# In an attention step, ScalarE copies the turned exponentials of two steps ago before it takes the last step's exponentials

## The chip, the cores and the metric

The kernel runs on one core of a Trainium2 chip. The metric is the device time of one execution in microseconds (us). A core has five engines that each work through a queue of their own in order: TensorE (PE, with its weight loads shown apart as PEld), VectorE (DVE), ScalarE (ACT), GpSimd (POOL) and SyncE (SP), which here only issues DMAs. Results of TensorE go to PSUM banks; everything else lies in SBUF.

## The reference: window attention, then a top-1 mixture of experts

Attention: 8 batches of 8 heads, 576 positions, head size 64. A query sees itself and the 63 positions before it:

```
scores = q @ k.T / 8, masked to 0 <= i - j < 64
attn   = exp(scores - max) / (sum + 1e-9)
x      = attn @ v            # 4608 rows of 512 after heads are joined
```

Mixture of experts: `logits = x @ w_gate` (8 experts), each row goes to its best expert, and gets `gate * relu(x @ w1[e]) @ w2[e]` with 1024 hidden columns.

## The kernel before

**Attention** comes first (about the first 160 us). It is cut into 36 steps of 128 rows, two chunks of 64 positions with all eight heads; q, k and v of a chunk are loaded into a ring of 18 slots by SP. The program is written out by hand as one loop over a step number i (lines 831 to 903), and in each turn of it the parts of several steps stand side by side:

- `scores(i)` (L401, L404): PE writes the scores of step i into one of two double banks `s_b`.
- `folded(i)`, `largest(i)` (L411 to L420): DVE folds the two halves of the window into one block, and takes the negated row maxima `mxs`.
- `exps(i - 1)` (L428): ACT takes the exponentials of the step before, eight activations of 128x64, one a head, from `s_b` into the tile `pf`.
- `transp(i - 1)` (L433): PE turns them, four transposes into the one bank `t_b`.
- `evac(i - 2)` (L437): ACT copies `t_b`, with the turned exponentials of two steps ago, into the tile `tsb`.
- `apart(i - 2)` (L444): POOL multiplies `tsb` by two masks and so writes the two tiles `pm`, two instructions.
- `values(i - 3)` (L458): PE multiplies `pm` with v into the bank pair `x_b`; the first product of a head needs the first `pm`, the next one the second.
- `shares(i - 3)` (L464 to L468): DVE divides by the row sums into `xrow`, and SP writes that out.
- `rows_t(i - 4)`, `cols_t(i - 4)` (L475, L482): PE turns `xrow` of the step before that, and ACT copies it to `xT`, for the gate's logits, which follow every fourth step (L519).

On PE the order within a turn is scores, values, `rows_t`, `transp`, and every fourth time the logits. On DVE it is folding, maxima, shares, and after them pieces of the routing (L534 to L603) and, late in the phase, the low parts of the first experts' weights (`wlo`, L237). On ACT it is the exponentials, the copy of `t_b`, the copy of `xT`, and small pieces behind it (`whi`, L240). `t_b` is one bank: the transposes of a turn wait until the copy of the step before has been taken out of it. `s_b`, `pf`, `tsb` and `pm` each have two buffers.

**The experts** follow (160 us to the end): passes of 256 or 384 gathered rows through an expert's two matrices, on PE without a break, each product made of three with the values split into a high and a low part. From turn 36 on the first of these passes are interleaved with what is left of the attention.

The change touches only the order of three calls in the loop.

Of the kernel before, what the change touches and what calls it, by code (L numbers as in the profile page):

```python
# [118 lines left out]
def window_attention_then_top1_moe(ctx: ExitStack, tc: tile.TileContext, qkv, wall, wg, cst, out):  # L119
# [66 lines left out]
    def turn(t, u, xt, b=None):  # L186
        xh, xl = xt
        xp = (bank("xp") if b is None else b).rearrange("p (k t) -> p k t", k=4)
        for kk in range(4):
            nc.tensor.transpose(xp[:, kk], t[:, u, kk * P:(kk + 1) * P], ident)  # L190
        us = slice(u * P, (u + 1) * P)
        nc.scalar.copy(out=xh[:, :, us], in_=xp)
        nc.vector.tensor_tensor(out=xl[:, :, us], in0=xp, in1=xh[:, :, us], op=ALU.subtract)  # L193
# [3 lines left out]
    class Weights:  # L197
# [11 lines left out]
        def load(self):  # L209
            jj = self.loaded  # L210
            if jj == NJ // 2:
                return
            self.loaded += 1
            raw = self.raws[jj] = wr.tile([P, 2, 2 * C], F32, name="raw")
            ev = self.ev
            src = wall[ev, jj] if isinstance(ev, int) else wall[bass.ds(ev, 1), jj].rearrange("o p j f -> p (o j) f")
            if jj < self.spread:
                at, gap = QUARTERS[jj]
                quarters.extend((at + gap * k, raw[:, k // 2, k % 2 * C:(k % 2 + 1) * C],
                                 src[:, k // 2, k % 2 * C:(k % 2 + 1) * C]) for k in range(4))  # L220
            else:
                nc.sync.dma_start(out=raw, in_=src)
# [157 lines left out]
    def keep_busy(k):  # L380

        for _ in range(k):
            nc.tensor.matmul(x_b[:, 1].rearrange("p (k t) -> p k t", k=4), lhsT=ones, start=True, stop=True,
                             rhs=ones.unsqueeze(1).to_broadcast([P, 4, P]))
# [375 lines left out]
    def table(lo, hi):  # L760
        read(gathered(keep["said"], NT, hi - lo, t_b), hi - lo, idx_sb[:, lo:hi], gate_sb[:, lo:hi])
# [8 lines left out]
    def get(i):  # L770
        fetch(xg[i % 3], cols(idx_sb, passes[i]))

    def flip(i, blocks=None):
        for u in range(len(passes[i])) if blocks is None else blocks:
            if u == 0:
                xt[i] = columns(xw)
            if u < len(passes[i]):
                turn(xg[i % 3], u, xt[i])

    def open_weights(i):  # L780
        wts[i] = Weights(expert_of(passes[i][0]))

    def each(f, n):
        if 0 <= n < NS:
            f(n)
# [17 lines left out]
    def do(what):  # L803
        if rs_[what]:
            rs_[what], f = None, rs_[what]
            f()
# [3 lines left out]
    def forward(i, place):  # L810
        if i >= TURN:
            for _ in range(FORWARD[i > TURN][place]):
                next(early)

    def split_ahead():

        w = next((ew[e] for e in range(EARLY) if e in ew and ew[e].given < NJ), None)
        if w and not w.ready:
            w.ready.append(w.split_(lows=lows))

    def single(k):
        sp = ctx.enter_context(tc.tile_pool(name=f"sp{k}", bufs=1, space=PSUM, side=side[k]))
        return [sp.tile([P, C], F32, name=f"e_b{2 * k + h}") for h in range(2)]

    def due(i):
        while begin and begin[0][0] <= i:
            begin.popleft()[1]()

    with tc.manual_schedule():
        keep_busy(BUSY[0])  # L830
        for i in range(NS + LAST):
            for c in range(FIRST, 2 * NS):

                if c % 2 and i == (c - RING + 1) // 2 + 4:
                    load(c)
            if i == LOADW:
                ew[0] = Weights(0, len(QUARTERS))
            if i == SPLIT:
                ew[0].prepare(AHEAD, pieces)
            if i == TURN:  # L840
                ew[0].first = ew[0].split()

            rs_["step"] = i
            if slow and slow[0][0]:
                f = slow.popleft()[1]
                if f:
                    f()
            if i <= TURN:
                due(i)
            each(exps, i - 1)  # L850
            each(evac, i - 2)
            each(apart, i - 2)
            if i == TURN:
                scored[1].close()
                turns["hp"] = single(1)
            while exs:
                exs.popleft()()
            if i > 5 and settled:
                settled.popleft()()
            if i > TURN:  # L860
                split_ahead()
            forward(i, 0)
            do("first")
            each(scores, i)
            each(folded, i)
            each(largest, i)
            if i < len(BUSY) - 1:
                keep_busy(BUSY[i + 1])
            forward(i, 1)
            each(values, i - 3)  # L870
            if i > TURN:
                due(i)
            for c in range(FIRST, 2 * NS):
                if c % 2 == 0 and i == (c - RING) // 2 + 3:
                    load(c)
            if quarters and quarters[0][0] <= i:
                _, o, w = quarters.popleft()
                nc.sync.dma_start(out=o, in_=w)
            if rs_["fast"] and (rs_["fast"][0][0] < i):
                rs_["fast"].popleft()[1]()  # L880
            forward(i, 2)
            each(rows_t, i - 4)
            each(cols_t, i - 4)
            forward(i, 3)
            each(transp, i - 1)
            do("last")
            each(shares, i - 3)
            do("read")
            if i == TURN - 1:
                scored[0].close()  # L890
                turns.update(xp=[t_b], yp=single(0))
                for u in range(2):
                    turn(xg[0], u, xe[0], turns["yp"][u])
            for k in range(RATE[0] if i < NS else 4):
                if slow and not slow[0][0]:
                    slow.popleft()[1]()
            for k in range(RATE[1] if i < NS else 4):
                if puts and not slow:
                    puts.popleft()()
            while lows:  # L900
                lows.popleft()()
            if pieces:
                pieces.popleft()()
        assert not (rs_["fast"] or slow or begin), (len(rs_["fast"]), len(slow), len(begin))
        while puts:
            puts.popleft()()
        st.close()
        xw = ctx.enter_context(tc.tile_pool(name="xw", bufs=2))
        xn = ctx.enter_context(tc.tile_pool(name="xn", bufs=1))
        turns["xp"].append(m_b)  # L910
        turns["yp"] = [x_b[:, 0], x_b[:, 1], *turns["yp"]]


        def steps():
            for _ in plan():
                for _ in range(WAIT[0]):
                    yield
            for _ in range(WAIT[1]):
                yield
            table(0, NMA)  # L920
            while "turned" not in keep:
                yield
            get(0)
            yield
            open_weights(0)
            get(1)

        rest = steps()
        for e, j in early:
            next(rest, None)  # L930
            if e == EARLY - 1 and j == NJ - 3:
                for _ in rest:
                    pass
            if e == EARLY - 1 and j is not None and j >= NJ - 3:
                flip(0, [j - NJ + 3])
# [62 lines left out]
```

## Time and profile before

| | |
|---|---|
| median of 3 runs | 649.79 us (648.19 to 986.33) |
| the profiled execution | 648.77 us, of which the span from first to last instruction is 647.0 us |
| PE busy, span | 612.2 us, 95% |
| ACT, DVE, POOL busy | 361.8, 397.5, 196.9 us |
| mean granted TensorE clock | 0.995 |

A row of a timeline gives the start, the duration, the engine, the line of the kernel and the operation with its output and input; several instructions of a kind that follow each other are one row (x64). In brackets stands how long the engine was idle before, and what ended that. Where it says "issue", the profile shows nothing that the engine waited for.

### The profile page before, as it was taken

Reading aid. Unit: us, or ns where it says so; the run is one execution under the profiler, and the core shown is the slowest. Engines: PE = TensorE matmul, PEld = TensorE weight load, DVE = VectorE, ACT = ScalarE, POOL = GpSimd, SP = SyncE. Lnnn points to the kernel's source line nnn. Section 1 sums busy time; section 2 is a strip of 40 time slices with the busy share of each in tenths; the row PEclk is TensorE's granted clock in tenths of the full one; section 3 lists DMA queues with packets and bytes.
Section 4 is the critical chain, followed back from the end, with each engine's and each line's share of the span. In section 5 each row is a group of like instructions: output and inputs, shape, how many; then the busy total and the mean of one; then the engine's idle time right before and its main releaser. Section 6 shows DMA issues by size and latency. Waiting matters only on the chain.

```text
span 647.0 us, 16938 instructions
## 1 busy us (share of the span) xinstructions
PE 612.2 (95%) x6995; PEld 542.6 (84%) x6995; DVE 397.5 (61%) x707; ACT 361.8 (56%) x763; POOL 196.9 (30%) x180
## 2 busy tenths in 40 slices
PE   8799988888989999999999999999999999999995
PEld 4688877777877899899899999999999999999994
DVE  4566769976789665744455556556556565655651
ACT  4576767675444455635345565565655655566551
POOL 4666657675521331401113122121211211111011
PEclk9999999999999999999999999999999999999999
DMA  9988888952645668634546666665666666555521
GB/s 304 345 274 263 295 262 264 314 172 100 247 146 194 212 206 296 221 137 140 180 162 224 218 224 235 204 223 208 226 226 210 223 236 225 210 182 187 212 98 34
DMA packets 35110, 138.13 MB, mean 213 GB/s; under 512 B 4940, under 2 KB 6092, under 8 KB 25552
## 3 DMA queue, kind: packets, MB, share of 16 engines
q1 hardware_dynamic: 28624, 118.08, 53.6%
q0 software_dynamic: 6400, 18.88, 8.4%
q8 instruction: 57, 0.93, 0.6%
q14 instruction: 29, 0.24, 0.1%
HBM read 119.11 MB, written 19.92 MB: 215 GB/s over the span
## 4 chain that ended last, share of the span: by engine, by line
PE 74%; DVE 12%; issue 9%; ACT 2%; POOL 2%; another core or an unknown queue 0%; POOLq 0%; DVEq 0%; ACTq 0%
PE e_b L307 20%; PE e_b L278 14%; PE x_b L278 14%; PE e_b L311 10%; PE x_b L458 4%; PE s_b L401 4%; DVE wlo L237 2%; PE m_b L475 2%; DVE s_b L418 1%; DVE s_b L412 1%; DVE xrow L468 1%; PE m_b L519 1%; PE t_b L190 1%; PE t_b L433 1%; PE m_b L190 1%
## 5 line engine op out<-in xcount | busy, mean ns | idle before, releaser
L237 DVE TENSOR_TENSOR wlo<-raw,whi 128x1024 fp32r<-128x1024 f32 (+1 forms) x158 | 188.6, 1194 | 165.7 <-ACT whi L240 153.1
L240 ACT CAST whi<-raw 128x1024 fp32r<-128x1024 f32 (+1 forms) x153 | 155.1, 1015 | 106.6 <-PE x_b L278 54.8
L307 PE MATMUL e_b<-xh,whi 128*128 128x256 f32 (+1 forms) x480 | 127.2, 294 | 0.0
L307 PE MATMUL e_b<-xl,whi 128*128 128x256 f32 (+1 forms) x480 | 125.0, 289 | 0.2 <-DVE xl L193 0.2
L444 POOL TENSOR_TENSOR pm<-tsb,cs 128x512 f32<-128x512 f32 x72 | 90.4, 1278 | 55.3 <-ACT tsb L437 48.5
L317 ACT ACTIVATE hh<-e_b 128x256 fp32r<-128x256 f32 (+1 forms) x152 | 60.4, 397 | 82.2 <-PE e_b L311 79.1
L307 PEld LDWEIGHTS e_b<-xl,whi 128*128 128x128 f32 x480 | 90.8, 189 | 4.1 <-DVE xl L193 0.6
L307 PEld LDWEIGHTS e_b<-xh,whi 128*128 128x128 f32 x480 | 90.8, 189 | 3.6
L267 POOL DMA_INDIRECT out<-ys,idx_sb x32 | 38.4, 1201 | 177.5 <-ACT ys L266 173.0
L179 POOL DMA_INDIRECT xg<-xs,idx_sb x32 | 35.2, 1099 | 180.9 <-PE m_b L190 127.9
L311 PE MATMUL e_b<-xh,wlo 128*128 128x256 f32 (+1 forms) x480 | 79.7, 288 | 0.0
L318 DVE SCALAR_TENSOR_TENSOR hl<-e_b,hh 128x256 fp32r<-128x256 f32 (+1 forms) x152 | 65.6, 432 | 15.3 <-ACT hh L317 14.7
L428 ACT ACTIVATE pf<-s_b,mxs 128x64 f32<-128x64 f32 x288 | 63.1, 339 | 9.7 <-DVE mxs L420 7.9
L311 PEld LDWEIGHTS e_b<-xh,wlo 128*128 128x128 f32 x480 | 67.7, 188 | 0.0
L278 PE MATMUL x_b<-whi,hh 128*128 128x512 f32 x160 | 62.9, 393 | 0.8 <-ACT ys L266 0.8
L278 PE MATMUL e_b<-whi,hl 128*128 128x512 f32 x160 | 62.8, 393 | 0.6 <-DVE hl L318 0.6
L278 PE MATMUL x_b<-whi,hl 128*128 128x512 f32 x160 | 62.8, 392 | 0.3 <-DVE hl L318 0.2
L278 PE MATMUL x_b<-wlo,hh 128*128 128x512 f32 x160 | 62.8, 393 | 0.0
L278 PE MATMUL e_b<-wlo,hh 128*128 128x512 f32 x160 | 62.8, 393 | 0.0
L278 PE MATMUL e_b<-whi,hh 128*128 128x512 f32 x160 | 62.7, 392 | 0.0
L458 PE MATMUL x_b<-ring,pm 64*64 64x65 f32 x2176 | 48.2, 224 | 14.1 <-issue 8.5
L458 PEld LDWEIGHTS x_b<-ring,pm 64*64 64x64 f32 x2176 | 42.5, 135 | 20.0 <-issue 13.9
(160 smaller groups left out, 886.6 us busy)
## 6 DMA issues: line engine op xcount, KB each, us to landing
raw<-wall SPq DMA_DIRECT2D x74, 1024.0 KB, 5.4
ring<-qkv SPq DMA_DIRECT2D x66, 386.0 KB, 4.4
xs<-xrow SPq DMA_DIRECT2D x36, 256.0 KB, 3.8
raw<-wall SPq DMA_DIRECT2D x8, 256.0 KB, 5.9
ring<-qkv SPq DMA_DIRECT2D x4, 256.0 KB, 4.8
ring<-qkv SPq DMA_DIRECT2D x4, 130.0 KB, 5.1
ring<-qkv SPq DMA_DIRECT2D x1, 512.0 KB
xg<-xs,idx_sb POOLq DMA_INDIRECT x32
```

The costliest lines, as they stand in the source:

```text
L179: nc.gpsimd.indirect_dma_start(out=t[:, u], out_offset=None, in_=xs[0:rows], in_offset=bass.IndirectOffsetOnAxis(ap=ix, axis=0), bounds_ch ...
L237: nc.vector.tensor_tensor(out=lo[:, s], in0=raw[:, s], in1=hi[:, s], op=ALU.subtract)
L240: nc.scalar.copy(out=hi[:, s], in_=raw[:, s])
L267: ins = nc.gpsimd.indirect_dma_start(out=out, out_offset=bass.IndirectOffsetOnAxis(ap=ix, axis=0), in_=ys, in_offset=None, bounds_check=N ...
L278: nc.tensor.matmul(y, lhsT=x[:, us], rhs=w[:, C:], start=(j == 0 and m == 0), stop=(j == NJ - 1 and m == 2))
L307: nc.tensor.matmul(hp[:, 0:w], lhsT=hi[:, ks], rhs=x[:, kk, 0:w], start=(kk == 0 and x is xh), stop=False)
L311: nc.tensor.matmul(hp[:, 0:w], lhsT=lo[:, kk * P:(kk + 1) * P], rhs=xh[:, kk, 0:w], start=False, stop=(kk == 3))
L317: nc.scalar.activation(out=hh[:, 0:w], in_=hp[:, 0:w], func=AF.Relu)
L318: nc.vector.scalar_tensor_tensor(out=hl[:, 0:w], in0=hp[:, 0:w], scalar=0.0, in1=hh[:, 0:w], op0=ALU.max, op1=ALU.subtract)
L428: nc.scalar.activation(out=pf[:, g, a], in_=sp[:, a, g, 0], func=AF.Exp, bias=mx[:, h:h + 1], scale=SCALE)
L444: nc.gpsimd.tensor_tensor(out=pm[i], in0=t.rearrange("p (g q) -> p g q", g=NG), op=ALU.mult, in1=cc("mask")[:, i * P:(i + 1) * P].unsqueez ...
L458: nc.tensor.matmul(x_b[cols, a, g * V1:(g + 1) * V1], lhsT=pm[i][rows, g, cols], rhs=v_r[rows, c % RING - i, g], start=(i == 0), stop=(i = ...
```

## The change

The copy of `t_b` and the two multiplications behind it are called ahead of the exponentials.

```diff
             if i <= TURN:
                 due(i)
-            each(exps, i - 1)
             each(evac, i - 2)
             each(apart, i - 2)
+            each(exps, i - 1)
             if i == TURN:
                 scored[1].close()
```

ACT's queue in a turn is then: the copy of `t_b`, the eight exponentials, the copy of `xT`. No instruction is added or taken away, and no other engine's queue has another order.

## Rows read from the trace of the kernel before

**Rows 1.** The page's first part: busy us, share of the span, instructions.

```profile
PE 612.2 (95%) x6995; PEld 542.6 (84%) x6995; DVE 397.5 (61%) x707; ACT 361.8 (56%) x763; POOL 196.9 (30%) x180
```

**Rows 2.** Stretches of 10 us: busy us (instructions) by engine, clock, DMA share, GB/s.

```profile
20.00:30.00 10.00, 6.24 (x190) 5.31 (x192) 5.55 (x14) 5.63 (x21) 5.62 (x5) 0.97 1.00 383
...
70.00:80.00 10.00, 9.62 (x306) 8.21 (x308) 7.93 (x21) 8.12 (x30) 6.13 (x5) 1.00 0.87 294
...
120.00:130.00 10.00, 8.90 (x246) 7.85 (x248) 9.17 (x21) 7.65 (x29) 6.18 (x5) 1.00 0.92 310
```

**Rows 3.** Waits in the first 175 us: us in total, times, longest.

```profile
POOL pm L444 <- ACT tsb L437: 48.5, 26, 8.0
...
PE x_b L458 <- POOL pm L444: 2.8, 4, 0.9
...
ACT tsb L437 <- PE t_b L433: 0.3, 1, 0.3
```

**Rows 4.** Timeline of ACT in one attention step.

```profile
77.31 0.59 ACT L482 COPY xT<-m_b 128x512 f32<-128x512 f32 x1 [0.75 <-PE m_b L475]
77.80 1.76 ACT L428 ACTIVATE pf<-s_b,mxs 128x64 f32<-128x64 f32 x8
79.38 0.65 ACT L437 COPY tsb<-t_b 128x512 f32<-128x512 f32 x1
```

**Rows 5.** Timeline of POOL in that step, and in one at 124 us.

```profile
80.11 2.51 POOL L444 TENSOR_TENSOR pm<-tsb,cs 128x512 f32<-128x512 f32 x2 [0.96 <-ACT tsb L437]
...
123.92 2.75 POOL L444 TENSOR_TENSOR pm<-tsb,cs 128x512 f32<-128x512 f32 x2 [3.00 <-ACT tsb L437]
```

**Rows 6.** Timeline of PE: values and transposes of several steps.

```profile
15.27 1.03 PE L458 MATMUL x_b<-ring,pm 64*64 64x65 f32 x40 [0.78 <-POOL pm L444]
...
18.68 1.04 PE L458 MATMUL x_b<-ring,pm 64*64 64x65 f32 x56 [0.57 <-POOL pm L444]
...
44.75 1.42 PE L458 MATMUL x_b<-ring,pm 64*64 64x65 f32 x64 [0.49 <-DVE xrow L468]
...
48.49 1.15 PE L458 MATMUL x_b<-ring,pm 64*64 64x65 f32 x61 [0.17 <-issue]
...
64.10 1.11 PE L458 MATMUL x_b<-ring,pm 64*64 64x65 f32 x64
...
75.21 1.48 PE L458 MATMUL x_b<-ring,pm 64*64 64x65 f32 x64
...
77.11 0.60 PE L433 MATMUL t_b<-cs,pf 128*128 128x128 f32 x4
...
78.87 1.38 PE L458 MATMUL x_b<-ring,pm 64*64 64x65 f32 x64
...
80.67 0.60 PE L433 MATMUL t_b<-cs,pf 128*128 128x128 f32 x4
...
112.86 1.27 PE L458 MATMUL x_b<-ring,pm 64*64 64x65 f32 x64
...
126.73 1.03 PE L458 MATMUL x_b<-ring,pm 64*64 64x65 f32 x40 [0.91 <-POOL pm L444]
```

**Rows 7.** Stretches of 1 us around the longest stall, columns as in Rows 2.

```profile
28.00:29.00 1.00, 0.00 (x0) 0.00 (x0) 0.34 (x2) 0.09 (x1) 1.00 (x1) 1.00 1.04 324
29.00:30.00 1.00, 0.46 (x17) 0.46 (x20) 0.00 (x0) 0.00 (x0) 1.00 (x2) 0.68 0.69 273
...
32.00:33.00 1.00, 1.00 (x16) 0.67 (x18) 0.00 (x0) 1.00 (x5) 0.00 (x0) 0.61 0.73 222
```

**Rows 8.** The chain that ended last: start, us, what.

```profile
125.55 1.41 DVE wlo L237
```

**Rows 9.** DVE by shape, 85 to 165 us: count, busy us, mean ns, idle.

```profile
L603 DVE TENSOR_TENSOR hot_row<-rowb,lo 128x512 bf16<-128x512 bf16 x7 | 5.3, 777 | 0.1
L237 DVE TENSOR_TENSOR wlo<-raw,whi 128x256 fp32r<-128x256 f32 x8 | 5.1, 638 | 0.1
```

**Rows 10.** Timeline of DVE: the same instruction twice.

```profile
121.75 0.42 DVE L237 TENSOR_TENSOR wlo<-raw,whi 128x256 fp32r<-128x256 f32 x1
...
125.48 1.48 DVE L237 TENSOR_TENSOR wlo<-raw,whi 128x256 fp32r<-128x256 f32 x1
```

## The prediction, made before the changed kernel was built or run

> **What bounds the kernel now.** I read the page first. PE is busy for 95% of the span [rows 1], and the change touches only the attention steps, some 160 of 647 us, so what it can be worth is read there. The table of busy time by stretches comes next [rows 2]; three regimes are to be seen in it. From 20 to 30 us the DMA engines are full (share 1.00) and PE has work for only 6.24 of 10 us. From 70 to 80 us PE is busy for 9.62 us and nothing else is close. From 120 to 130 us DVE is at 9.17 and PE at 8.90.
>
> Then the list of waits [rows 3]. POOL waits 48.5 us for the copy of the turned exponentials, which looks like much, but POOL's idleness is no cost by itself. What PE shows as a wait for POOL's masked tiles is 2.8 us in four places; that is the number the change can work on.
>
> Last the timelines, of one step. ACT copies `xT` at 77.31, takes eight exponentials from 77.80 and copies `t_b` at 79.38 [rows 4], although the transposes that filled `t_b` ended at 77.71 (77.11 and 0.60) [rows 6]. So the copy lies ready for 1.67 us and waits its turn. POOL follows at 80.11 and is done at 82.62 [rows 5]. The values of a step take 1.11 us on PE where nothing holds them (64.10), and 1.38 and 1.48 us in the steps around 75 and 79 [rows 6]: in the middle of them PE waits for the second masked tile. Such short waits are too small for the list, and I count them below.
>
> **The change, part by part.** One ACT copy of 0.65 us moves ahead of eight activations of 1.76 us together [rows 4]. Nothing is added or removed. The two POOL instructions move in program text with it, but no other POOL instruction stands between the old and the new place, so POOL's order is the same; SP, DVE and PE are not touched either, and no DMA is issued in what is moved.
>
> *What comes earlier.* The copy starts when the transposes have ended, or the `xT` copy ahead of it: 77.80 in the step shown, not 79.38, so 1.58 us earlier. The masked tiles come earlier by as much wherever POOL waits for the copy. No wait of PE for the second tile in rows 6 that I can see in a plain step is longer than 1.58 us, so all of them go, as far as something else is not late next.
>
> *The first steps.* PE waits 0.78 us at 15.27 and 0.57 us at 18.68 [rows 6], 1.35 us together. But the next 10 us are those with full DMA engines and a PE that is idle for over a third [rows 2]. A PE that arrives earlier there waits longer for what the DMAs bring. The bounds are 0 and 1.35 us; I take 0.4, nearer to the lower end, since the share of 1.00 says that the transfers set the pace.
>
> *The stretch where PE sets the pace, 40 to 115 us.* The excess over 1.11 us is 0.31 (44.75), 0.04 and an idle 0.17 (48.49), 0.37 (75.21), 0.27 (78.87) and 0.16 (112.86) [rows 6]: 1.3 us. Other steps are within 0.1 us of the 1.11. I take 1.3, with 0.6 as the lower bound (half, if DVE's rows of the step before hold the values next, as they do for 0.49 us at 44.75).
>
> *The stretch where DVE sets the pace, 85 to 105 and 120 to 150 us.* At 126.73 PE waits 0.91 us for POOL [rows 6], but the chain of what ended last runs over DVE there (the 1.41 us at 125.55) [rows 8], so I count nothing; the cover is DVE's own work, and without it this would be 0.9 us more of gain.
>
> *What comes later.* The exponentials end later by the copy ahead of them, 0.49 us from start to start if that is spaced as 77.31 to 77.80, at most 0.65. Who waits: the transposes at the end of the same PE turn. In the step shown the exponentials end at 79.56 and would end at 80.05 to 80.21; the transposes start at 80.67 [rows 4, 6]. If the values ahead of them lose their 0.27 us of waiting, they start at 80.40, so 0.2 to 0.35 us are left. The transposes wait today for the copy and the exponentials both, whichever is last, and their sum on ACT is the same. Taken at nothing; the bounds are 0 and the whole 1.3 us (it can give the gain back, not more, because in the old order the same two pieces end at 80.03).
>
> *The new wait.* The copy now stands at the head of ACT's turn and can hold the exponentials back until PE has finished the transposes. They ended at 77.71 and ACT became free at 77.80; and where they were late before, the copy waited 0.3 us in one place of 36 [rows 3]. Behind it on ACT stand eight exponentials and the `xT` copy; with the slack above this costs nothing, at most 0.1 us a step over the 11 or so tightest ones, 1 us.
>
> *DVE and POOL side by side.* The same `wlo` instruction takes 0.42 us at 121.75 and 1.48 us at 125.48 [rows 10]; POOL's masking ran from 123.92 to 126.67 [rows 5], and the slow one ended soon after it. So one of the two holds the other up, and the change shifts POOL by 1.6 us against DVE. The Trainium skill, SBUF — State Buffer, "Who interferes with whom", says that a DVE instruction with two inputs in SBUF and a GpSimd instruction that reads SBUF exclude each other for a whole instruction; by that rule alone the sum could come out on the other side, and it is the third case below. The trace agrees: 1.06 us is near what is left of a masking instruction of about 1.26 us, half of 2.51. From the rows: 15 such instructions (8 `wlo`, 7 `hot_row`) took 10.4 us [rows 9]; at 0.42 and, for `hot_row`, my estimate of 0.69 (its mean of 0.777 less about 0.09 for the one or two that look held) they would take 8.2, so 2.2 us are paid today. Bounds: the 2.2 go, or each of 15 waits half a masking instruction, 0.63 us, 9.4 in all, 7.2 more than today. I take no change: at 121.6 the copy would start in place of the exponentials and POOL at about 122.3, when the `wlo` of 121.75 has just ended, and the one of 125.48 would find POOL done; elsewhere it can go the other way.
>
> *Sum.* 0.4 + 1.3 = 1.7 us less than the profiled execution's 648.77 (span 647.0): 647.1 us. That execution stands 1.0 us below the median shown and 0.6 above the lowest run, so I hold it for typical.
>
> **The rivals.** (1) *Nothing reaches the end.* DMA takes the front, DVE and the exponentials take the rest: 648.8 us. For it speaks that the end of the exponentials has only 0.2 to 0.35 us of slack, against it the plain excess in steps where PE has nothing else to wait for.
>
> (2) *More goes than I count.* The whole 1.35 of the front, 1.3, the 0.9 at 126.73, and the 2.2 of DVE: 5.8 us, 643.0. Also the clock: after the stall at 28 us, in which PE ran nothing, the granted clock fell to 0.68, and it was 0.61 in the fourth 1 us stretch from there [rows 7]; if the stall shrinks so that the fall does not come, the missing shares of two of these stretches alone are 0.7 us, near 1.5 for the four as an estimate. Then 641.5. A fall more costs as much: 648.6 in my forecast.
>
> (3) *POOL collides with DVE: slower.* Place: 85 to 165 us, where after the shares DVE has its two-input instructions. They come at the end of DVE's turn, and POOL's two instructions would now start about 0.75 us after the transposes, where today they start 2.4 us after them. The price is 0.63 us for each of 15, 7.2 us over today, less the 1.7: 654.3. It decides where such an instruction starts after POOL has, not before. In the step at 121.75 it is before by some 0.1 us; that is thin. For over 2% each would have to wait for a whole masking instruction: 15 x 1.26 is 18.9, less 2.2 and 1.7 gives 15 us, 663.8; little speaks for that.
>
> **How the numbers follow.** Forecast (645 to 648): 0.48. Rival 1 (648 to 650): 0.22. Rival 2 (640 to 645): 0.15. Rival 3 (650 up): 0.15. The time is the forecast's, 647.1. The range leaves out the lower part of rival 2 and the upper of rival 3, about 0.1 each, and so goes from 642.0 to 652.0. 2%, about what a measurement tells from no change, is 13 us; below it I see 0.015 (all of rival 2 twice over) and above it 0.02 (rival 3 at full price). Within: 0.965.
>
> **What would show it.** In the changed kernel's timeline the copy of `t_b` starts where the exponentials do now, POOL starts within 0.8 us of the end of the transposes, and POOL's wait for the copy shifts, not shrinks. PE's listed wait for POOL, 2.8 us, goes to under 1, and values of a plain step take 1.11 us. The plain step from transposes to transposes, 3.56 us at 77 to 81, should be near 3.3. I am wrong if PE waits for exponentials in many steps (rival 1), if the two-input instructions of DVE take clearly more than 10.4 us together (rival 3), or if the attention phase as a whole ends over 4 us earlier (rival 2).

## The result, and the profile after it

The changed kernel takes 657.39 us in the median of 4 runs (655.74 to 659.93); the kernel before, run beside it, 649.45. The ratio is 1.0148, with an interval of 1.0124 to 1.0172: 1.5% slower by this ratio, 1.2% by the two medians, where 647.1 us and a range of 642 to 652 were forecast. The ratios leave out two executions that stand far off, one of the kernel before (986.33 us) and one of an experiment (1511.14 us). A second series gave 1.0149 [1.0108, 1.0191]. The profiled execution took 658.86 us (span 657.0), 10.1 more than the profiled one before.

ACT does what was intended. Its timeline in a step of the changed kernel (columns as in [rows 4]):

```profile
46.74 0.59 ACT L482 COPY xT<-m_b 128x512 f32<-128x512 f32 x1 [0.90 <-PE m_b L475]
47.23 0.59 ACT L437 COPY tsb<-t_b 128x512 f32<-128x512 f32 x1
47.72 1.55 ACT L428 ACTIVATE pf<-s_b,mxs 128x64 f32<-128x64 f32 x7
```

The copy starts 0.09 us after the transposes (46.54 + 0.60); in [rows 4, 6] it lay 1.67 us. PE in the same step:

```profile
46.54 0.60 PE L433 MATMUL t_b<-cs,pf 128*128 128x128 f32 x4
...
47.99 1.11 PE L458 MATMUL x_b<-ring,pm 64*64 64x65 f32 x64
...
49.53 0.60 PE L433 MATMUL t_b<-cs,pf 128*128 128x128 f32 x4
```

The values take the undisturbed 1.11 us; transposes to transposes is 2.99 us, where the same step took 3.48 before (46.59 to 50.07). So this plain step is shorter. The list of waits in the first 185 us (us in total, times, longest) says what is late instead:

```profile
POOL pm L444 <- ACT tsb L437: 53.5, 27, 6.7
PE x_b L458 <- DVE xrow L468: 9.6, 10, 1.6
...
PE x_b L554 <- DVE xrow L468: 5.9, 2, 4.0
ACT tsb L437 <- PE t_b L433: 4.0, 4, 1.8
PEld t_b L433 <- ACT pf L428: 2.2, 7, 0.7
PE x_b L458 <- POOL pm L444: 1.0, 1, 1.0
```

PE's wait for POOL fell from 2.8 to 1.0 us [rows 3] (its weight loads, which take the same masked tiles, show 7.6 us, 5.3 before; four of these seven places lie at a wait of PE for the row), but in the two lines in which it waits for DVE's `xrow` stand 15.5 us together, 4.8 before. What makes `xrow` late is in DVE's instructions by shape, 85 to 170 us (count, busy us, mean ns, idle), which answer to [rows 9]:

```profile
L237 DVE TENSOR_TENSOR wlo<-raw,whi 128x256 fp32r<-128x256 f32 x8 | 11.6, 1453 | 0.0
L603 DVE TENSOR_TENSOR hot_row<-rowb,lo 128x512 bf16<-128x512 bf16 x7 | 5.8, 848 | 0.1
L539 DVE SCALAR_TENSOR_TENSOR eq<-ld,cs 128x128 f32<-128x128 f32 x1 | 1.2, 1242 | 0.0
L537 DVE TENSOR_TENSOR ld<-lgs,lm 128x128 f32<-128x128 f32 x1 | 1.2, 1205 | 0.0
L614 DVE TENSOR_TENSOR here<-mid,cs 128x64 bf16<-128x64 f32 x1 | 1.1, 1129 | 0.0
```

The same 15 instructions (8 `wlo`, 7 `hot_row`) take 17.4 us where they took 10.4. The three pieces of routing below them took 0.29, 0.29 and 0.21 us before. DVE's timeline, an undisturbed one, a held one and the worst one:

```profile
122.43 0.41 DVE L237 TENSOR_TENSOR wlo<-raw,whi 128x256 fp32r<-128x256 f32 x1
...
126.68 1.50 DVE L237 TENSOR_TENSOR wlo<-raw,whi 128x256 fp32r<-128x256 f32 x1
...
148.89 3.48 DVE L237 TENSOR_TENSOR wlo<-raw,whi 128x256 fp32r<-128x256 f32 x1
```

POOL's timeline, where the held ones lie. The worst one started 0.71 us before the first masking, while POOL ran an indirect DMA (a gather of rows), and ended 0.28 us after the second masking:

```profile
125.41 2.49 POOL L444 TENSOR_TENSOR pm<-tsb,cs 128x512 f32<-128x512 f32 x2 [3.46 <-PE s_b L401]
...
148.57 1.00 POOL L179 DMA_INDIRECT xg<-xs,eidx  x1 [0.30 <-issue]
149.60 2.49 POOL L444 TENSOR_TENSOR pm<-tsb,cs 128x512 f32<-128x512 f32 x2
```

And PE behind it:

```profile
155.01 0.21 PE L554 MATMUL x_b<-oh,tri 128*128 128x104 bf16 x1 [3.97 <-DVE xrow L468]
...
155.53 1.99 PE L401 MATMUL s_b<-ring 64*64 64x128 f32 x32
157.29 1.75 PE L458 MATMUL x_b<-ring,pm 64*64 64x65 f32 x64
```

PE stands still for 3.97 us, and then the scores take 1.99 us instead of 1.10 and the values 1.75 instead of 1.11. The stretches of 1 us show why (columns as in [rows 2]; the clock is the one behind POOL's busy time):

```profile
154.00:155.00 1.00, 0.00 (x0) 0.00 (x0) 0.90 (x2) 0.00 (x0) 0.00 (x0) 1.00 0.00 0
155.00:156.00 1.00, 0.99 (x21) 0.97 (x24) 0.00 (x0) 0.36 (x2) 0.00 (x0) 0.64 0.19 74
156.00:157.00 1.00, 1.00 (x28) 1.00 (x24) 0.00 (x0) 1.00 (x5) 0.55 (x1) 0.50 0.49 188
157.00:158.00 1.00, 1.00 (x40) 1.00 (x36) 0.35 (x1) 1.00 (x5) 1.00 (x2) 0.50 0.00 0
158.00:159.00 1.00, 1.00 (x49) 0.93 (x41) 0.97 (x2) 0.02 (x1) 0.95 (x1) 0.66 0.06 16
```

The granted clock falls to 0.50, the lower of the two levels, 1.2 GHz, once PE runs again. It does so a second time at 166 to 168 us. Summed over 86 to 176 us the missing shares are 3.4 us; before they were 0. The chain of what ended last, 140 to 165 us, runs through the same place (start, us, what):

```profile
148.97 3.40 DVE wlo L237
...
154.27 0.70 DVE xrow L468
...
155.60 1.92 PE s_b L401 x32
157.52 1.53 PE x_b L458 x64
```

### The profile page after: what moved, and what is told of

It reads as the page before. It is cut to its first block, busy times and chain, and to the rows that moved or that the text cites. A ratio compares the mean times of both kernels' runs of the same rounds, so it can differ in the third digit from the quotient of the medians.

```text
span 657.0 us, 16937 instructions
## 1 busy us (share of the span) xinstructions
PE 611.8 (93%) x6995; PEld 543.1 (83%) x6995; DVE 405.5 (62%) x707; ACT 362.2 (55%) x763; POOL 198.4 (30%) x180
## 4 chain that ended last, share of the span: by engine, by line
PE 71%; DVE 14%; issue 10%; POOL 3%; ACT 2%; POOLq 0%; ACTq 0%; DVEq 0%
PE e_b L307 19%; PE e_b L278 14%; PE x_b L278 14%; PE e_b L311 10%; PE x_b L458 3%; DVE wlo L237 3%; PE s_b L401 3%; PE m_b L475 2%; POOL pm L444 2%; DVE s_b L418 2%; DVE s_b L412 1%; DVE xrow L468 1%; PE m_b L519 1%; PE t_b L190 1%; PE m_b L190 1%
## 5 line engine op out<-in xcount | busy, mean ns | idle before, releaser
L237 DVE TENSOR_TENSOR wlo<-raw,whi 128x1024 fp32r<-128x1024 f32 (+1 forms) x158 | 195.2, 1236 | 164.8 <-ACT whi L240 162.4
L444 POOL TENSOR_TENSOR pm<-tsb,cs 128x512 f32<-128x512 f32 x72 | 92.0, 1300 | 57.5 <-ACT tsb L437 53.5
L458 PE MATMUL x_b<-ring,pm 64*64 64x65 f32 x2176 | 45.3, 223 | 18.6 <-DVE xrow L468 9.6
```

Source lines behind the costliest of these rows:

```text
L237: nc.vector.tensor_tensor(out=lo[:, s], in0=raw[:, s], in1=hi[:, s], op=ALU.subtract)
L444: nc.gpsimd.tensor_tensor(out=pm[i], in0=t.rearrange("p (g q) -> p g q", g=NG), op=ALU.mult, in1=cc("mask")[:, i * P:(i + 1) * P].unsqueez ...
L458: nc.tensor.matmul(x_b[cols, a, g * V1:(g + 1) * V1], lhsT=pm[i][rows, g, cols], rhs=v_r[rows, c % RING - i, g], start=(i == 0), stop=(i = ...
```

## The experiments

The median alone can't say where time is lost: in the first half of the attention each execution has stalls of PE that the profile calls "issue", 1.7 to 4.5 us between 30 and 85 us in six executions with the old order in those turns and 2.8 to 5.6 in seven with the new one. So beside each ratio stands a **lag**: the start of the transposes in PE's timeline, minus the start of the same ones in the profiled execution before (88.99 us for step 20, 158.72 for step 35). What is added to it between these two steps is free of the first half. Three kernels that start POOL late in these turns and add no work (new up to 20, held, before with pieces left out) have -2.3 to -0.9 there; it scatters by a microsecond or two. A lag is that of one execution: for the held maskings the slowest of its kernel (652.76 us), for the kernels "up to turn 31" and "PE filled" the fastest.

| kernel | ratio, interval | lag, step 20 | step 31 | step 33 | step 35 | added, 20 to 35 |
|---|---|---|---|---|---|---|
| changed | 1.0148 [1.0124, 1.0172] | +2.6 | +6.0 | +3.8 | +9.6 | +7.0 |
| changed, again | 1.0149 [1.0108, 1.0191] | +1.5 | +6.0 | +5.0 | +8.3 | +6.8 |
| new order up to turn 20 | 0.9999 [0.998, 1.0018] | +1.7 | +1.8 | -0.6 | 0.0 | -1.7 |
| new order from turn 21 | 1.0076 [1.0051, 1.01] | +0.4 | +1.5 | +0.6 | +3.8 | +3.4 |
| maskings held back | 1.0007 [0.9988, 1.0025] | +5.0 | +5.6 | +3.2 | +4.1 | -0.9 |
| changed, pieces left out | 1.0069 [1.0035, 1.0102] | +3.4 | +3.1 | +1.0 | +6.6 | +3.2 |
| before, pieces left out | 1.0006 [0.9976, 1.0037] | +1.4 | +1.3 | 0.0 | -0.9 | -2.3 |
| before, a reading more | 1.0077 [1.006, 1.0094] | 0.0 | +3.7 | +2.6 | +5.2 | +5.2 |
| before, fills more | 1.0128 [1.011, 1.0146] | +1.2 | +4.0 | +5.5 | +6.4 | +5.2 |
| new order up to turn 31 | 1.0077 [1.0044, 1.011] | +1.7 | +1.5 | +1.7 | +1.7 | 0.0 |
| new order from turn 32 | 1.0055 [1.0034, 1.0076] | +1.9 | +1.5 | +3.3 | +4.3 | +2.4 |
| changed, PE filled | 1.0121 [1.0091, 1.0152] | -0.6 | +5.2 | +3.5 | +5.8 | +6.4 |

Three theories stood at first. P: POOL's maskings, now earlier, meet DVE's two-input instructions, and only the second half, where DVE has these, loses. Q: the loss comes of ACT's order itself, with the exponentials behind the copy, and so evenly over all turns. F: it is made in the first half, where PE in the profiled execution was some 3 us behind by step 17. (Comments in the code cuts below are added here.)

**Half of the turns.** The new order in the first turns alone, and in the last alone:

```diff
-            each(evac, i - 2); each(apart, i - 2); each(exps, i - 1)
+            if i <= 20:      # the second kernel: if i > 20
+                each(evac, i - 2); each(apart, i - 2); each(exps, i - 1)
+            else:
+                each(exps, i - 1); each(evac, i - 2); each(apart, i - 2)
```

> The new order in turns 0 to 20 of the loop, the old one from turn 21 on; nothing else differs. Theory P (the loss is VectorE held up by GpSimd's masking, in the turns where VectorE has instructions with two inputs in SBUF, 21 and later): 647.5 to 650.5 us, as the old order or up to the 1.3 us better that the forecast counted in the plain steps. Theory F (the loss is made in the first half, where PE stood 2.8 us behind the old order at the transposes of step 17): 651.5 to 653 us. Theory Q (the loss comes from the exponentials being later on ScalarE, in every step alike): about half, 652 to 654 us.

> The other half: the old order in turns 0 to 20, the new one from turn 21 on. Theory P: 655 to 658 us, the whole loss. Theory F: 652 to 655 us, what the second half adds. Theory Q: 652 to 654 us.

The first 21 turns lose nothing (647.73 us), which speaks against Q and F; they gain nothing either. In that kernel the eight pieces of `wlo` come off better than before, by shape, 85 to 170 us:

```profile
L603 DVE TENSOR_TENSOR hot_row<-rowb,lo 128x512 bf16<-128x512 bf16 x7 | 5.3, 777 | 0.1
L237 DVE TENSOR_TENSOR wlo<-raw,whi 128x256 fp32r<-128x256 f32 x8 | 3.3, 416 | 0.3 <-ACT whi L240 0.3
```

The other half loses 0.76%, half of the whole: the two don't add to 1.48. Its 652.56 us miss what P expected and lie where Q and F had it, so the halves alone don't decide.

**ACT's new order, POOL's old start.** POOL first reads one column of the last exponential, and so can't start before ACT has done all eight; on ACT the copy stays ahead.

```diff
             each(evac, i - 2)
+            each(exps, i - 1)
+            each(held, i - 1)     # POOL copies pf[:, NG - 1, 1, 0:1]
             each(apart, i - 2)
-            each(exps, i - 1)
```

> The new order on ScalarE in all turns, but GpSimd first reads one column of the last exponential (one instruction of 128x1 more a step on GpSimd), so its masking starts behind the exponentials, within 0.5 us of where it started in the old order. Theory P: the loss goes, 648 to 651 us; the 8 low-part pieces of 128x256 take 4 to 6 us together again, not 11.6. Theory Q: the exponentials are as late as in the changed kernel, so 655 to 659 us. Theory F: 651 to 654 us if its cause is on ScalarE or PE.

1.0007 [0.9988, 1.0025]: the loss is gone, with ACT's order unchanged from the slow kernel, and PE's two waits for `xrow` are 6.7 us, not 15.5. So it is not the exponentials' place that costs, but when POOL starts. DVE by shape, same stretch:

```profile
L606 DVE TENSOR_TENSOR hot_row<-rowb,lo 128x512 bf16<-128x512 bf16 x7 | 5.4, 796 | 0.1
L237 DVE TENSOR_TENSOR wlo<-raw,whi 128x256 fp32r<-128x256 f32 x8 | 5.3, 658 | 0.1
```

10.7 us, where before had 10.4 and the changed kernel 17.4. POOL and DVE in one of its steps:

```profile
136.59 0.18 POOL L431 COPY hold<-pf 128x1 f32<-128x1 f32 x1 [1.15 <-ACT pf L428]
136.72 2.51 POOL L447 TENSOR_TENSOR pm<-tsb,cs 128x512 f32<-128x512 f32 x2
```

```profile
138.40 0.69 DVE L471 TENSOR_TENSOR xrow<-x_b,rs 128x512 f32<-128x512 f32 x1
139.00 0.51 DVE L237 TENSOR_TENSOR wlo<-raw,whi 128x256 fp32r<-128x256 f32 x1
```

The maskings end at 139.23, and a `wlo` from 139.00 is done 0.28 us later. On this run the verdict rests. Its granted clock is 1.00 from 86 us on.

**Fewer victims.** In both orders the eight low pieces become fills, which read nothing.

```diff
                 nc.scalar.copy(out=hi[:, s], in_=raw[:, s])
-                low(s)
+                if pieces is None: low(s)
+                else: nc.vector.memset(lo[:, s].bitcast(F32), 0.0)
```

> The new order, and the 8 pieces of 128x256 of the first weights' low part (L237) are set to zero in place of the subtraction: the low part of two blocks is left out, the instruction on VectorE stays but has no input. To be read against the old order with the same edit. Theory P: of the loss of 8 us the 6.5 us that these pieces grew by go, and the 3.3 us that they cost by themselves: 647 to 650 us. Theory Q: only the 3.3 us by themselves go, 653 to 656 us.

> The old order with the same edit as n_new_no_low: the 8 pieces of the low part are set to zero, the subtraction is left out. Theory P: they cost 5.1 us here and mostly on the chain between 110 and 150 us, so 644 to 647 us, and the new order with the edit stays 5 to 7 us behind, since other instructions with two inputs (oh, eq, hot_row) now meet the masking there. Theory Q: 8 to 10 us behind, as without the edit.

Both missed what P expected: the new order's 653.39 us lie in Q's range, the old order's 648.15 above P's. In the old order the pieces' 2.9 us on DVE come back as nothing. In the new order the loss against that kernel falls from 1.5% to about 0.6%, not to nothing, and its trace shows other two-input instructions meeting the maskings. DVE by shape, 85 to 170 us, in the changed kernel without the pieces:

```profile
L552 DVE TENSOR_TENSOR oh<-eq,em 128x96 bf16<-128x96 f32 x1 | 3.2, 3241 | 0.0
...
L542 DVE SCALAR_TENSOR_TENSOR eq<-ld,cs 128x128 f32<-128x128 f32 x1 | 1.2, 1245 | 0.0
L542 DVE SCALAR_TENSOR_TENSOR eq<-ld,cs 128x96 f32<-128x96 f32 x1 | 1.2, 1216 | 0.0
```

The `oh` started at 145.90 and ended at 149.14, 0.12 us after a pair of maskings that began at 146.52 and took 2.50; undisturbed it takes 0.26. It too had started before the maskings, in an indirect DMA of POOL (145.50 to 146.50). The missing shares of the clock are 3.4 us in sum from 86 to 176 us, as in the changed kernel.

**The changed kernel once more**, beside the following two.

> The changed kernel itself again, beside the others. All theories: 1.010 to 1.017 of the old order. What it tells is how the profile scatters: by theory P the 8 pieces and 7 hot_row take 15 to 19 us together again; the 2.8 us that PE had lost by the transposes of step 17 are scatter if they are gone or of another size here.

The same ratio, by other collisions: `wlo` 8.5 us, not 11.6, but `oh` 2.10 and both `eq` 1.24 and 1.27. `wlo` and `hot_row` together take 14.2 us, under the 15 to 19 expected. Which instruction is hit changes from one execution to the next; the lag added is +6.8 and +7.0.

**The old order with more work on POOL.** Behind the maskings of turns 21 to 35 stands one more multiplication like them, which reads SBUF, or three fills, which only write.

```diff
+            if 21 <= i <= 35:
+                extra(i - 2)   # one tensor_tensor of tsb and the mask;
+                               # the other kernel: three memsets of 128x512
```

> The old order, and in turns 21 to 35 GpSimd does one more multiplication of 128x512 like a masking (it reads the same tile and mask in SBUF, and its output is not used), behind the two. No other engine waits for it. Theory P: VectorE's two-input instructions that follow the shares meet it, up to 1.26 us each: 5 to 9 us slower than the old order, 653 to 657 us, and over 4 us slower than x_write. Rival W (it is GpSimd's being busy that delays the routing or the next masking, not its reading): both x kernels slower alike, by 2 to 5 us. Theory Q: neither moves, 647 to 649 us.

> As x_read, but the addition on GpSimd is three fills of 128x512 with zero (about 1.3 us together by the 4.0 us that three fills of 128x1536 take at the start of the profile), which write SBUF and read none of it. Theory P with the rule of the Trainium skill, SBUF - State Buffer, section Who interferes with whom (only a GpSimd instruction that reads SBUF excludes a two-input VectorE instruction): 647 to 650 us, as the old order. Rival W: as slow as x_read.

As a pair this failed: P expected 653 to 657 us with the reading and 647 to 650 with the fills; they came to 652.99 and 655.73. The fills make POOL late for what follows: the changed waits, 85 to 185 us, are `DVE lo L593 <- POOL mid L589`, 4.0 us (2.4 before), and 4.9 us of PE for the masked tiles (1.5 before). Rival W, POOL's being busy, is nearer to these times, but in the changed kernel POOL is early, not late. So the pair doesn't price the collision. It shows it by the instruction, though. DVE and POOL with the fills, at 142 us:

```profile
142.35 0.26 DVE L544 TENSOR_TENSOR ld<-lgs,lm 128x96 f32<-128x96 f32 x1
142.64 0.26 DVE L546 SCALAR_TENSOR_TENSOR eq<-ld,cs 128x96 f32<-128x96 f32 x1
142.82 0.42 DVE L237 TENSOR_TENSOR wlo<-raw,whi 128x256 fp32r<-128x256 f32 x1
```

```profile
142.04 1.69 POOL L452 MEMSET more<- 128x512 f32 x3
```

Three two-input instructions run through 1.69 us of fills, all undisturbed, where POOL's multiplications, which read, hold them up. With the reading one, an `oh` took 3.01 us, through the rest of a masking, the next one and the added multiplication, a `said` 1.48 and a `here` 1.19 (undisturbed 0.26, 0.48 and 0.21).

**The last turns.** The halves again, cut at turn 31.

```diff
-            if i <= 20:
+            if i <= 31:      # the other kernel: if i > 31
```

> The new order in turns 0 to 31, the old one in 32 to 36. Theory P with C: the two long stalls of PE come from turns 33 to 36, where VectorE waited through two maskings (3.48 us for one piece); they and the half clock go, and what is left is the 4 us or so that VectorE had lost by turn 31: 650.5 to 653 us, no half clock after 100 us. Theory Q (every turn alike): 655.5 to 657.5 us.

> The reverse: the old order in turns 0 to 31, the new one in 32 to 36. Theory P with C: the two stalls and the half clock come back, 652 to 655 us. Theory Q: 5 of 36 turns, 648.5 to 649.5 us.

The profiled execution of the first was its fastest, 650.55 us, and its `wlo` took 3.4 us, near the 3.3 of eight undisturbed ones; its ratio stands at 1.0077, so its lags tell little of its other executions. P's 650.5 to 653 us missed: the median is 655.44, at the lower edge of what Q had. The five last turns alone cost 0.55% (653.6 us, as P expected), and their trace has the changed kernel's pattern in small. DVE and PE:

```profile
147.42 2.10 DVE L549 TENSOR_TENSOR oh<-eq,em 128x96 bf16<-128x96 f32 x1
```

```profile
147.37 1.71 PE L458 MATMUL x_b<-ring,pm 64*64 64x65 f32 x48 [2.60 <-DVE xrow L468]
149.01 1.11 PE L475 MATMUL m_b<-cs,xrow 128*128 128x128 f32 x4
149.91 1.06 PE L433 MATMUL t_b<-cs,pf 128*128 128x128 f32 x4
```

The `oh` comes behind the stall of 2.60 us; ahead of it an `eq` took 1.21 us at 142.02 and a `wlo` 1.49 at 143.15 (undisturbed 0.26 and 0.41). After that stall the clock is at half from 148 to 151 us, and 1.11 and 1.06 us stand for 0.66 and 0.60.

**The clock by itself.** In the changed kernel, PE gets products that nobody reads where it stood still in the profiled execution.

```diff
+            if i == 35:
+                keep_busy(14, m_b)
...
+            if i == 36:
+                keep_busy(5, t_b)
```

> The new order in all turns, and PE gets 14 products of 128x512 that nobody reads at the start of turn 35 (into m_b) and 5 in turn 36 (into t_b), in the two stalls at 151 to 155 and 163.5 to 165 us of the changed kernel, after which the granted clock was at half for 3.4 us' worth of PE time. VectorE and GpSimd do the same as in the changed kernel. Theory C (a part of the loss, 3.4 us, is the clock that falls after PE has stood still): the clock stays at 1.00 from 145 to 170 us and the time is 652 to 655 us, 3 to 4 us below the changed kernel's 656.9. Rival (the loss is all VectorE's, and the slow PE is hidden behind it): 656 to 659 us, with the clock at 1.00. In both the two-input instructions of VectorE take as long as in the changed kernel.

The stretch of 20 us that had a clock of 0.83 now has 1.00:

```profile
150.00:170.00 20.00, 19.00 (x354) 14.73 (x352) 10.91 (x34) 10.97 (x30) 11.17 (x15) 1.00 0.30 106
```

The time is the rival's, 656.9 us, not the 652 to 655 of theory C; the ratio is 1.0121 [1.0091, 1.0152] against 1.0148 [1.0124, 1.0172], and the intervals overlap. The run doesn't part the two. Its `wlo` (8.6 us) are held, but the long stall did not come: the piece at 148.09 took 0.42 us and the row was done at 151.08, while the first fill kept PE until 154.14 (3.18 us; the second takes 1.24). So here the fill cost PE some 3 us of its own, and the full clock may be due to the missing stall.

How much of the 1.5% is the clock stays open, but the mean clock of each execution sets a bound. The missing share times the span is 8.9 us in the mean of eight executions of the changed kernel (5.3 to 11.8; the profiled one is the lowest) and 3.2 in 61 of the kernel before; it is 3.4 with the maskings held, 7.2 with PE filled, and 6.7 and 8.2 with the added reading and the fills. So up to 5.7 of the 8 to 9 us lost can be a slower PE behind the stalls. It is a bound and not a price, since a slower PE costs nothing where another engine sets the pace.

## Why the prediction was wrong

**The step that failed** is the term "DVE and POOL side by side", taken at no change between -2.2 and +7.2 us. The 15 instructions went from 10.4 to 17.4 us: +7.0, at the upper end (in the second series +3.8, with other instructions held in their place). It was set by one step, at 121.75 and 125.48 us, in which the shift by 1.6 us seemed to free the later instruction. In the changed kernel that neighbourhood has `wlo` at 126.68 inside the maskings of 125.41 to 127.90. The sign stood in the timelines of the kernel before, as a count, had all eight pieces been laid beside the maskings:

```profile
117.58 0.42 DVE L237 TENSOR_TENSOR wlo<-raw,whi 128x256 fp32r<-128x256 f32 x1
```

```profile
118.42 1.26 POOL L444 TENSOR_TENSOR pm<-tsb,cs 128x512 f32<-128x512 f32 x1 [1.51 <-ACT tsb L437]
```

This piece ends 0.42 us before the next masking begins. Five of the eight are free, and end 0.42 to 1.75 us ahead of the next masking; four of these gaps are shorter than the 1.6 us by which the change brings POOL forward. The count came out, six of eight held and not three; piece by piece it did not. This second piece stayed free in the changed kernel (122.43), and the third, 1.75 us ahead of its masking, was held (126.68).

**Rival 3** was the case: its place, and its 7.2 us against 7.0 measured for the same 15. That the size agrees is partly luck: it let each of the 15 wait 0.63 us, and eight were held, by 0.5 to 3.1 us. Its total, 654.3, was 4.6 short of the profiled 658.86. The 1.7 us that it subtracted don't show. Routing's instructions, which it didn't count, gave another 1.3 (DVE's two-input instructions between 85 and 170 us, each less its shortest time in any run, lost 12.9 us to POOL in all, 4.6 before). And the clock fell behind the stalls, which stood in rival 2, for the front, and not here. The Trainium skill, SBUF — State Buffer, "Who interferes with whom", which supports the rival, has it that the one that comes first holds the shared pair for a whole instruction and that a GpSimd instruction that only writes doesn't contend; the 1.50 us and the undisturbed 0.42 through the fills agree. The 3.48 us don't: that `wlo` had started 0.71 us before the first masking, and both maskings went ahead of it; there the measurement stands. By the rival's own condition, that it decides where an instruction starts after POOL has, this piece would have been free.

**The first steps.** Of the waits of 0.78 and 0.57 us none is left for POOL; in their place PE waits 0.97 us for the load of q, k and v at 14.70 and 0.39 for DVE's row at 18.71. PE is busy for 6.34 us of the 10 from 20 us, 6.24 before [rows 2]. What was counted, 0.4, can't be told from the scatter.

**The stretch where PE sets the pace.** Plain steps are shorter as said (the one of 3.56 us takes 3.39, 80.10 to 83.49, where 3.3 was expected; values 1.11), but the 1.7 us of the sum don't reach the end: the kernel with the new order up to turn 20 stands at 0.9999, where 1.7 us would be 0.9974, just under its interval. The stalls called "issue" are as large as before or larger; that they took the gain is a guess. The fourth listed wait for POOL, 0.58 us at 91.57, is in no term of the sum.

**What would show it.** POOL's wait for the copy did shift, not shrink (48.5 to 53.5 us), POOL starts 0.76 us after the transposes (47.90), and PE's listed wait for POOL went to 1.0. The sign named for rival 3, clearly more than 10.4 us, is the one that came.

**Later exponentials** and **the new wait** were rightly costed at nothing: PE's weight loads for the transposes wait 2.2 us for `pf`, 1.8 before; ACT waits 4.0 us for the transposes, not 0.3, but the kernel with held maskings has 3.6 us of that wait and loses nothing. A wait that the prediction does not name came with the later exponentials: DVE's folding waits 8.6 us for them, and not at all before; with held maskings it is 7.2 and with the new order up to turn 20 8.6, and neither loses.

**DVE's stretch at nothing** was wrong with the same cause: DVE is busy for 58.01 of the 65 us from 85 us on, 53.22 before, and PE follows it.

**What stays open.** Why the parts cut at turn 20 don't add to the whole: up to 20 costs nothing and from 21 on 0.76%, although the parts cut at turn 31, 0.77% and 0.55%, add to 1.32, within the intervals. The instruction that is hit depends on how the step happens to lie, by tenths of a microsecond; that this makes the parts differ is argued, not shown. Nor is it shown what decides whether a waiting instruction of DVE goes between the two maskings or behind both, or what held the two worst ones before the first masking began. How much of the time is the clock is bounded only. No version tried is faster than the old order; new to turn 20 and held maskings equal it.

## What to carry to other kernels

Before an engine's work is made to start earlier, lay its new interval over the instructions of its neighbour that it can hold up, in every step, and count the ones that it would now cover; one step proves nothing. Price a collision by what stands behind the victim: a 1 us hold in front of the row that PE needs can be 1 us of PE, and a stall of some microseconds can cost the clock on top. A shorter wait in the list is worth only what the next releaser leaves of it: here PE waited 1.8 us less for POOL and 10.7 more for DVE's row.

## What the runs showed of the hardware

- A two-input DVE instruction can wait through two POOL multiplications in a row: 3.48 us for 0.41 (`wlo`), 3.24 and 2.10 for 0.26 (`oh`). The first two had started 0.71 and 0.62 us before the first of these, while POOL ran an indirect DMA; another two-input instruction in the same DMA as the first ran undisturbed (0.26 us at 148.72). POOL is held up as well, less: pairs of maskings took up to 3.10 us, not 2.50.
- After PE had stood still for 3.97, 2.74 and 2.60 us (the changed kernel, its second series, the new order from turn 32) the granted clock fell to half, 1.2 GHz, only once PE had work again, for some 3 us. The stall's length alone doesn't set it: the wait of 1.62 us for `lgT` stands in both kernels, and behind it the clock was 0.50 from 166 to 168 us in the changed one and 1.00 from 157 to 159 before. In the second series the same wait (165.09) and one of 2.28 us (149.87) left it at 1.00.
